# Five double blocks of a top-1 expert layer: first layer with the weights stationary and 256 tokens moving

## The chip, the core and the metric

One core of a Trainium2 chip runs the whole kernel as one launch. The metric is the device time of an execution in microseconds; several executions were timed, and one more was recorded by the hardware profiler.

## The reference

Three stages follow one another: attention with sink and window over 2 x 768 tokens and 8 heads; a mixture of 8 experts in which every token goes through every expert, weighted by a Sinkhorn matrix; and a second mixture in which each token goes to one expert only. The change is in the third stage:

```python
logits = x @ w_gate                      # x: 1536 x 512, 8 experts
expert_idx = np.argmax(logits, axis=1)
...
for e in range(E):
    mask = expert_idx == e
    xe = x[mask]
    h = np.maximum(xe @ w1[e], 0.0)      # first layer, 512 -> 1024
    ye = h @ w2[e]                       # second layer, 1024 -> 512
    out[mask] = gate_w[mask, None] * ye
```

## The kernel before

Every float32 operand of a matmul is kept as two parts, `hi` and `lo` (`lo = x - hi`), and a product is three matmuls into the same PSUM bank (`mm3`, lines 66 to 69): lo x hi, hi x lo, hi x hi. ScalarE (ACT in the rows) writes the hi part, VectorE (DVE) subtracts for the lo part.

**The third stage.** Tokens of one expert are gathered into blocks of 128 rows, numbered `i`. Blocks 0 and 1 belong to the expert with the most tokens. From 2 on blocks come in *turns* of three: 2, 5, 8, 11, 14, 17 stand alone (all but block 2 are *half* blocks of 64 rows, which carry hi and lo side by side in one operand and need two matmuls in place of three), and 3/4, 6/7, 9/10, 12/13, 15/16 are *pairs* (double blocks) with the same expert, so that they share its weights.

For a block the steps are:
- `gather(i)`: an indirect DMA issued on POOL fetches the rows (tile `acc`).
- `xs_trans(i)`: four transposes on TensorE into PSUM (`xst`, in the one buffer `m0`), the hi part by ACT, the lo part by DVE.
- `m2_l1(i, hf)`: half `hf` of the first layer. The token block is the stationary operand, 512 hidden columns of the weights move: 12 matmuls of 512 columns (8 for a half block) into PSUM bank `L0` or `L1`. The result, tokens by hidden, is read out with its ReLU by ACT (hf 0) or DVE (hf 1); for a half block ACT copies one part and DVE adds the other (`both`).
- `h_trans(i)`: eight transposes on TensorE (`h2p`) turn the hidden layer for use as the stationary operand, and ACT and DVE split it again, four parts each a pair.
- `m2_l2(i)`: 24 matmuls of 512 columns (16 for a half block) into `y`; for a half block ACT copies and DVE adds, then ACT scales by the gate, and POOL issues the scatter to the output.

**Weights.** Each expert needs four 1 MB tiles, loaded by SP into four raw buffers. `item_split` splits a tile in two *steps*: each is one ACT copy and one DVE subtraction of 128x1024 (`w_split`). There are 7 slots for split tiles; `spend(n)` issues up to n steps, if the slot is free (`uses`); `ensure` issues what a block needs at once; a finished split issues the load of the tile four places on. A turn uses eight tiles, 16 steps.

The order on every engine is the order in which the code is written (`manual_schedule`), and each engine works its instructions off in that order. The loop of the third stage, lines 1510 to 1525, is the order before:

```python
for i in range(2, NSURE):
    if i + 1 < NSURE:
        drain(m2_l1(i + 1, 0))
    ...
    spend(2 if i % 3 == 0 else 1)
    if i + 1 < NSURE:
        drain(m2_l1(i + 1, 1))
    spend(2)
    if i + 2 < NSURE:
        xs_trans(i + 2)
    spend(1)
    for n, _ in enumerate(m2_l2(i)):
        if n == 4 and i + 1 < NSURE:
            h_trans(i + 1)
```

Of the kernel before, what the change touches and what calls it, by code (L numbers as in the profile page):

```python
# [8 lines left out]
F32 = mybir.dt.float32  # L9
F32R = mybir.dt.float32r  # L10
# [13 lines left out]
def kernel(  # L24
# [62 lines left out]
    x2d = dram.tile([N, DM], F32, name="x2d")  # L87

    accp = ctx.enter_context(tc.tile_pool(name="accp", bufs=1))
    acc = [accp.tile([128, DM], F32, name=f"acc{i}") for i in range(NT)]  # L90
    xp = ctx.enter_context(tc.tile_pool(name="xp", bufs=1))
    hp_a = ctx.enter_context(tc.tile_pool(name="hp_a", bufs=1))
    xh = [xp.tile([128, KD, CH], F32R, name=f"xh{c}") for c in range(NC)]
# [24 lines left out]
    for t in range(NOVER):  # L118
        for j in range(2):
            FIRST[NSURE + 2 * t + j] = NSURE + 2 * t  # L120
            COL[NSURE + 2 * t + j] = 2 * t + j
    HALF = {2 + 3 * u for u in range(1, NONE)}

    def whose(i, rs):
        return [(i, r) for r in rs] if FIRST[i] == i else []
# [606 lines left out]
    def rows(i):  # L732
        return 64 if i in HALF else 128

# [7 lines left out]
    def gather(i):  # L742
# [4 lines left out]
        )  # L747
        xs_t[i] = x

    def xs_trans(i):  # L750
        x = xs_t.pop(i)
        n = rows(i)
        tp = pools["ps"].tile([128, KD, 128], F32, name="xst", tag="m0")[:, :, 0:n]
        for kk in range(KD):
            nc.tensor.transpose(tp[:, kk, :], x[0:n, kk * 128:(kk + 1) * 128], ident[0:n, 0:n])
        if i in HALF:

            st = stile("xsh", i, [128, KD, 128], F32R)
            nc.scalar.activation(st[:, :, 0:n], tp, AF.Copy)
            nc.vector.tensor_tensor(st[:, :, n:128], tp, st[:, :, 0:n].bitcast(F32), op=ALU.subtract)  # L760
            xst[i] = st, None
            return
        th = stile("xsh", i, [128, KD, 128], F32R)
        tl = stile("xsl", i, [128, KD, 128], F32R)
        nc.scalar.activation(th, tp, AF.Copy)
        nc.vector.tensor_tensor(tl, tp, th.bitcast(F32), op=ALU.subtract)
        xst[i] = th, tl

    def mm(out_ap, ah, al, bh, bl, start, stop):
        if al is not None:  # L770
            mm3(out_ap, ah, al, bh, bl, start, stop)
        else:
            nc.tensor.matmul(out_ap, ah, bl, start=start, stop=False)
            nc.tensor.matmul(out_ap, ah, bh, start=False, stop=stop)

    def both(dst, ps):

        nc.scalar.activation(dst, ps[64:128, :], AF.Copy)
        nc.vector.tensor_tensor(dst, ps[0:64, :], dst, op=ALU.add)

    def m2_l1(i, hf):
        if 2 <= i < NSURE:
            ensure(i, hf)
        th, tl = xst[i]
        wh, wl = w_t[pos[i, hf]]
        ps = ps_m.tile([128, HF], F32, name="L", tag=f"L{hf}")
        for kk in range(KD):
            a = None if tl is None else tl[:, kk, :]
            mm(ps, th[:, kk, :], a, wh[:, kk, :], wl[:, kk, :], kk == 0, kk == KD - 1)
            yield  # L790
        used(i, (hf,))
        h = h2[i, hf] = stile(f"h{hf}", i, [128, HF])
        if i in HALF:
            both(h[0:64, :], ps)
        elif hf == 0 or i < 2 or i == NSURE - 1:
            nc.scalar.activation(h, ps, AF.Relu)
        else:
            nc.vector.tensor_scalar(h, ps, 0.0, None, op0=ALU.max)

    def h_trans(i, hfs=(0, 1)):  # L800
        if hfs[0] == 0:
            h2t[i] = []
        for hf in hfs:
            n = rows(i)
            tp = pools["ps"].tile([128, FB, 128], F32, name="h2p", tag=f"y{1 + hf}")[:, :, 0:n]
            h = h2.pop((i, hf))
            for f in range(FB):
                nc.tensor.transpose(tp[:, f, :], h[0:n, f * 128:(f + 1) * 128], ident[0:n, 0:n])
            th = stile(f"hh{hf}", i, [128, FB, 128], F32R)
            if i in HALF:  # L810
                hi = th[:, :, 0:n]
                nc.scalar.activation(hi, tp, AF.Relu)
                nc.vector.scalar_tensor_tensor(
                    th[:, :, n:128], tp, 0.0, hi.bitcast(F32), op0=ALU.max, op1=ALU.subtract
                )
                h2t[i].append((th, None))
                continue
            tl = stile(f"hl{hf}", i, [128, FB, 128], F32R)
            nc.scalar.activation(th, tp, AF.Copy)
            nc.vector.tensor_tensor(tl, tp, th.bitcast(F32), op=ALU.subtract)  # L820
            h2t[i].append((th, tl))

    def m2_l2(i):
        pool, tag = ((ps_m, "y0"), (pools["ps"], "m2"))[i % 2]
        ps = pool.tile([128, DM], F32, name="y", tag=tag)
        for f in range(2 * FB):
            if f % FB == 0 and 2 <= i < NSURE:
                ensure(i, 2 + f // FB)
            th, tl = h2t[i][f // FB]
            wh, wl = w_t[pos[i, 2 + f // FB]]  # L830
            a = None if tl is None else tl[:, f % FB, :]
            mm(ps, th[:, f % FB, :], a, wh[:, f % FB, :], wl[:, f % FB, :], f == 0, f == 2 * FB - 1)
            if f % FB == FB - 1:
                used(i, (2 + f // FB,))
            yield
        y = stile("y", i, [128, DM])[0:rows(i), :]
        if i in HALF:
            both(y, ps)
            ps = y
        nc.scalar.activation(y, ps, AF.Copy, scale=index(g_s, g_d, i))  # L840
        nc.gpsimd.indirect_dma_start(  # L841
            out=out, out_offset=bass.IndirectOffsetOnAxis(ap=index(is_s, is_d, i), axis=0), in_=y, in_offset=None,
            bounds_check=N - 1, oob_is_err=False,
        )
# [4 lines left out]
    def spend(n):  # L849
        while n > 0:  # L850
            if not todo:
                m = head[0]
                if m >= NHEAD or (m >= len(SLOTS) and uses[m - len(SLOTS)] > 0):
                    return
                todo.append(item_split(m))
                head[0] += 1
            try:
                next(todo[0])
                n -= 1
            except StopIteration:  # L860
                todo.pop(0)
# [523 lines left out]
    def tick():  # L1385
        for job in list(jobs):
            job[0] -= 1
            if job[0] <= 0:
                try:
                    w = next(job[1])  # L1390
                    job[0] = 4 if w is None else w
                except StopIteration:
                    jobs.remove(job)

    with tc.manual_schedule():
# [50 lines left out]
        def hand_over():  # L1446
            raw2.extend(p.tile([128, FB, 512], F32, name="raw", tag="raw") for p in (raw_a, raw_b, raw_c, raw_c))
            s0 = (NG - 1) * NC * FB
            hs = [((hp_a if j < 4 else hp_b), j) for j in ((s0 + t) % 6 for t in range(6))]
            free = [(p, f"h{x}{j}") for p, j in hs for x in "hl"]  # L1450
            a = [(accp, f"acc{j}") for j in range(NT)]
            small.update(xs=[a[0], a[1], a[8]], xsh=a[3:5], xsl=a[5:7], R=[a[2], a[7]], y=a[9:11])
            small.update(h0=free[8:12:2], h1=free[9:12:2])
            for j, key in enumerate(("hh0", "hl0", "hh1", "hl1")):
                small[key] = [free[j], free[4 + j]]

        for g in range(NG):
            for c in range(NC):
# [23 lines left out]
        def mix(gen):  # L1482
            for _ in gen:
                tick()
# [5 lines left out]
        for i in range(2):  # L1490
            mix(m2_l1(i, 0))
            for n, _ in enumerate(m2_l1(i, 1)):
                tick()
                if n == 0:
                    h_trans(i, (0,))
            h_trans(i, (1,))
            for n, _ in enumerate(m2_l2(i)):
                tick()
                if n == 5:
                    while i + 1 not in xs_t:  # L1500
                        tick()
                    xs_trans(i + 1)
        mix(m2_l1(2, 0))
        xs_trans(3)
        mix(m2_l1(2, 1))
        while jobs:
            tick()
        h_trans(2)
        spend(4)
        for i in range(2, NSURE):  # L1510
            if i + 1 < NSURE:
                drain(m2_l1(i + 1, 0))
            if i + 3 < NSURE:
                gather(i + 3)
            spend(2 if i % 3 == 0 else 1)
            if i + 1 < NSURE:
                drain(m2_l1(i + 1, 1))
            spend(2)
            if i + 2 < NSURE:
                xs_trans(i + 2)  # L1520
            spend(1)
            for n, _ in enumerate(m2_l2(i)):
                if n == 4 and i + 1 < NSURE:
                    h_trans(i + 1)
            spend(1 if i < NSURE - 2 else 8)
        more = nc.values_load(mo_i[0:1, 0:1], min_val=0, max_val=NOVER)  # L1526

        def over(t):
# [53 lines left out]
```

## Time and profile before

| | us |
|---|---|
| median of 3 timed executions | 1448.63 (1448.29 to 1449.07) |
| the profiled execution, its own time | 1447.51 |
| its span, first to last instruction | 1445.3 |
| TensorE busy in it | 1406.3 |
| VectorE busy | 684.6 |
| ScalarE busy | 454.1 |
| GpSimd (POOL) busy | 130.2 |

The profiled execution's time is its span and 2.2 us around it. Busy times are sums over stages that are very different: attention in the first 200 us, the first expert layer up to about 1210 us, then the routing and the blocks of the second expert layer. PE in the rows is TensorE's matmuls, PEld its weight loads, which lie beside the matmuls. The duration of a matmul in a row reaches to the end of its result and overlaps the next; how often one can follow another is read from the starts.

### The profile page before, as it was taken

How to read it: one execution, taken by the hardware profiler on the slowest of the kernel's cores; microseconds unless marked ns; L12 is line 12 of the kernel's file. 1: busy time of each engine (PE TensorE's matmuls, PEld its weight loads, DVE VectorE, ACT ScalarE, POOL GpSimd, SP SyncE). 2: the span in 40 equal slices, each digit the busy share in tenths (PEclk: the TensorE clock that was granted, in tenths of full speed). 3: DMA queues.
4: the chain of work that ended last, by engine and by line, in shares of the span. 5: the costliest groups of instructions: out<-in, count | busy, mean ns of one | idle time of the engine just before them, and what ended most of it. 6: DMA issues, size and time to landing. Idle time of an engine off the chain costs nothing. (4 is left out here: it accounts for less than half of the span.)

```text
span 1445.3 us, 17989 instructions
## 1 busy us (share of the span) xinstructions
PE 1406.3 (97%) x7101; PEld 1150.3 (80%) x7101; DVE 684.6 (47%) x1369; ACT 454.1 (31%) x895; POOL 130.2 (9%) x172
## 2 busy tenths in 40 slices
PE   7799999999999999999999999999999999899997
PEld 5587887888888888888888888888888877688885
DVE  7777644543333323232433333242323257877884
ACT  5766522021121112020221112020221123477774
POOL 3644400000000000000000000000000000212221
PEclk9999999999999999999999999999999999999999
DMA  6322112010101000010101000010100041797782
GB/s 131 78 59 53 38 59 87 1 59 1 59 0 59 29 29 30 29 59 0 58 0 59 30 30 30 30 58 0 58 1 0 15 161 37 248 319 276 271 291 71
DMA packets 85707, 105.01 MB, mean 73 GB/s; under 512 B 41358, under 2 KB 41358, under 8 KB 85616
## 3 DMA queue, kind: packets, MB, share of 16 engines
q1 hardware_dynamic: 83056, 96.58, 20.2%
q0 software_dynamic: 2560, 7.21, 1.4%
q8 instruction: 58, 0.95, 0.3%
q14 instruction: 33, 0.27, 0.1%
HBM read 100.63 MB, written 7.21 MB: 75 GB/s over the span
## 5 line engine op out<-in xcount | busy, mean ns | idle before, releaser
L210 ACT ACTIVATE hh<-L 128x512 fp32r<-128x512 f32 x192 | 114.7, 597 | 794.9 <-PE L L69 794.8
L211 DVE SCALAR_TENSOR_TENSOR hl<-L,hh 128x512 fp32r<-128x512 f32 x192 | 132.8, 692 | 345.5 <-ACT hh L210 344.8
L235 DVE SCALAR_TENSOR_TENSOR acc<-y,Pm,acc 128x512 f32<-128x512 f32 x168 | 126.1, 751 | 252.3 <-PE y L69 251.9
L67 PE MATMUL y<-whb,hl 128*128 128x512 f32 x416 | 164.8, 396 | 0.0
L67 PE MATMUL y<-wha,hl 128*128 128x512 f32 x412 | 163.2, 396 | 0.0
L69 PE MATMUL y<-whb,hh 128*128 128x512 f32 x416 | 162.2, 390 | 0.0
L68 PE MATMUL y<-wlb,hh 128*128 128x512 f32 x416 | 162.1, 390 | 0.0
L69 PE MATMUL y<-wha,hh 128*128 128x512 f32 x412 | 160.6, 390 | 0.0
L68 PE MATMUL y<-wla,hh 128*128 128x512 f32 x412 | 160.5, 390 | 0.0
L67 PE MATMUL L<-xh,wla 128*128 128x512 f32 x384 | 152.2, 396 | 0.0
L67 PE MATMUL L<-xh,wlb 128*128 128x512 f32 x384 | 150.9, 393 | 0.0
L68 PE MATMUL L<-xl,wha 128*128 128x512 f32 x384 | 149.6, 389 | 0.0
L69 PE MATMUL L<-xh,wha 128*128 128x512 f32 x384 | 149.6, 389 | 0.0
L68 PE MATMUL L<-xl,whb 128*128 128x512 f32 x384 | 149.5, 389 | 0.0
L69 PE MATMUL L<-xh,whb 128*128 128x512 f32 x384 | 149.5, 389 | 0.0
L745 POOL DMA_INDIRECT acc<-x2d,ig_s x2 | 2.1, 1048 | 1044.2 <-DVE tmp_d L458 1019.1
L69 PEld LDWEIGHTS y<-whb,hh 128*128 128x128 f32 x416 | 78.1, 188 | 16.6
L67 PEld LDWEIGHTS y<-whb,hl 128*128 128x128 f32 x416 | 78.1, 188 | 15.7
L67 PEld LDWEIGHTS y<-wha,hl 128*128 128x128 f32 x412 | 77.3, 188 | 16.5 <-issue 0.2
L68 PEld LDWEIGHTS y<-wlb,hh 128*128 128x128 f32 x416 | 78.2, 188 | 15.3
L69 PEld LDWEIGHTS y<-wha,hh 128*128 128x128 f32 x412 | 77.3, 188 | 16.3
L68 PEld LDWEIGHTS y<-wla,hh 128*128 128x128 f32 x412 | 77.4, 188 | 14.8
(346 smaller groups left out, 2297.0 us busy)
## 6 DMA issues: line engine op xcount, KB each, us to landing
raw<-in_moe_w SPq DMA_DIRECT2D x80, 1024.0 KB
raw<-in_v SPq DMA_DIRECT2D x12, 256.0 KB
raw<-vfb SPq DMA_DIRECT2D x12, 256.0 KB
x2d<-acc SPq DMA_DIRECT2D x12, 256.0 KB
raw<-in_k SPq DMA_DIRECT2D x11, 256.0 KB
raw<-in_q SPq DMA_DIRECT2D x11, 256.0 KB
raw<-in_k SPq DMA_DIRECT2D x2, 128.0 KB
raw<-in_q SPq DMA_DIRECT2D x2, 128.0 KB
```

The costliest lines, as they stand in the source:

```text
L67: nc.tensor.matmul(out_ap, al, bh, start=start, stop=False)
L68: nc.tensor.matmul(out_ap, ah, bl, start=False, stop=False)
L69: nc.tensor.matmul(out_ap, ah, bh, start=False, stop=stop)
L210: nc.scalar.activation(hh, ps, AF.Relu)
L211: nc.vector.scalar_tensor_tensor(hl, ps, 0.0, hh.bitcast(F32), op0=ALU.max, op1=ALU.subtract)
L235: nc.vector.scalar_tensor_tensor(a, ps, Pm[:, blk, e:e + 1], a, op0=ALU.mult, op1=ALU.add)
L745: nc.gpsimd.indirect_dma_start(out=x[0:rows(i), :], out_offset=None, in_=src, in_offset=bass.IndirectOffsetOnAxis(ap=index(ig_s, ig_d, i), ...
```

## The change

A pair's first layer is computed with the roles exchanged: 128x128 tiles of the weights are stationary and the 256 tokens of the pair move, so that the result comes out hidden by tokens, as the second layer wants it. A new `pair_l1(i, hf)` does both blocks of a pair at once, in two *units* for each half: 24 matmuls of 256 columns into one bank (`L0`, `L1` in turn), then one ACT ReLU (hi) and one DVE step (lo). The pair has no `h_trans` any more. The hidden tiles of a pair take eight buffers, `xpair` holds the pair's transposed tokens in two tiles of 256 columns (two pairs of `acc` buffers are joined for it). Half blocks and block 2 keep the old form.

The loop is written by *units of work*: the half block's first layer, or the pair's, is issued one place ahead of its second layer; the transposes of the gathered blocks two places ahead; split steps stand behind the pair's units (2 each, 8), in the pair's second layers (3 each, 6), in the half block's second layer (2) and behind its two first-layer halves (1 each, 2).

```diff
+        if i in PAIR or i - 1 in PAIR:
+            js = slice(0, 128) if i in PAIR else slice(128, 256)
+            th, tl = (t[:, :, js] for t in xpair[i if i in PAIR else i - 1])
+            nc.scalar.activation(th, tp, AF.Copy)
+            nc.vector.tensor_tensor(tl, tp, th.bitcast(F32), op=ALU.subtract)
+            return
...
+    def pair_l1(i, hf):
+
+        ensure(i, hf)
+        th, tl = xpair[i]
+        wh, wl = w_t[pos[i, hf]]
+        for u in range(2):
+            ps = ps_m.tile([128, 2, 256], F32, name="L", tag=f"L{u}")
+            for j in range(2):
+                fs = slice((2 * u + j) * 128, (2 * u + j + 1) * 128)
+                for kk in range(KD):
+                    mm3(ps[:, j, :], wh[:, kk, fs], wl[:, kk, fs], th[:, kk, :], tl[:, kk, :], kk == 0, kk == KD - 1)
+            if u == 1:
+                used(i, (hf,))
+                used(i + 1, (hf,))
+            n = 2 * (2 * hf + u)
+            hh, hl = (stile("hp", n + j, [128, 2, 256], F32R) for j in range(2))
+            nc.scalar.activation(hh, ps, AF.Relu)
+            nc.vector.scalar_tensor_tensor(hl, ps, 0.0, hh.bitcast(F32), op0=ALU.max, op1=ALU.subtract)
...
+            yield
...
+        def turn(i):
+
+            xs_trans(i)
+            if i + 3 < NSURE:
+                gather(i + 3)
+
+        gather(5)
         mix(m2_l1(2, 0))
-        xs_trans(3)
+        turn(3)
         mix(m2_l1(2, 1))
         while jobs:
             tick()
+        turn(4)
         h_trans(2)
-        spend(4)
-        for i in range(2, NSURE):
...
+        spend(3)
+        units = [(2,)]
+        for i in sorted(PAIR):
+            units += [(i, i + 1), (i + 2,)]
+        for n, u in enumerate(units):
+            v, w = (units[n + k] if n + k < len(units) else () for k in (1, 2))
+            for hf in range(2):
+                if len(v) == 2:
+                    for _ in pair_l1(v[0], hf):
+                        spend(2)
+                elif v:
+                    drain(m2_l1(v[0], hf))
+                    spend(1)
+                for i in w[hf:hf + 1]:
+                    turn(i)
+            for i in u:
+                for k, _ in enumerate(m2_l2(i)):
+                    if k == 4 and i == u[-1] and len(v) == 1:
+                        h_trans(v[0])
+                    if k in ((1, 3, 6) if len(u) == 2 else (2, 5)):
+                        spend(1)
+            if n == len(units) - 2:
+                spend(8)
```

How this moves instructions, first on TensorE, from the gathered block 9 on. `xst` are the transposes of gathered blocks, `h2p` those of the hidden layer, `L` is the first layer, `y` the second; the number behind a name is that of its buffer's use. Before: xst of block 9, second layer of block 7 with the half block 8's h2p in it, first layer of block 9, xst of block 10, second layer of block 8, in it block 9's h2p (rows that only repeat are left out):

```order
L755 MATMUL xst<-ident,acc_10856 128x128 x4
L67 MATMUL y<-xh_10767,hl_10922 128x512
L68 MATMUL y<-xl_10768,hh_10921 128x512
L69 MATMUL y<-xh_10767,hh_10921 128x512
...
L808 MATMUL h2p<-ident,hh_10959 128x64 x4
L808 MATMUL h2p<-ident,hl_10978 128x64 x4
...
L67 MATMUL L<-wha_10896,acc_10994 128x512
L68 MATMUL L<-wla_10897,acc_10993 128x512
...
L755 MATMUL xst<-ident,acc_10962 128x128 x4
L773 MATMUL y<-xl_10985,hh_11020 128x512
...
L808 MATMUL h2p<-ident,hh_11073 128x128 x4
L808 MATMUL h2p<-ident,hl_11092 128x128 x4
```

Now: the half block 8's xst between the units of the pair 6/7 (256 columns, weights stationary), then, behind the second layer of block 5, the two halves of block 8's first layer, each with one xst of the next pair (block 9, block 10) behind it, and only then block 6's second layer:

```order
L67 MATMUL L<-acc_10624,wla_10596 128x256
L68 MATMUL L<-acc_10625,wha_10595 128x256
L69 MATMUL L<-acc_10624,wha_10595 128x256
L764 MATMUL xst<-ident,acc_10499 128x64 x4
L67 MATMUL L<-acc_10624,wla_10649 128x256
...
L789 MATMUL L<-whb_10885,acc_10850 128x512
L764 MATMUL xst<-ident,acc_10633 128x128 x4
L788 MATMUL L<-wla_10922,acc_10850 128x512
L789 MATMUL L<-wha_10921,acc_10850 128x512
...
L764 MATMUL xst<-ident,acc_10659 128x128 x4
L67 MATMUL y<-xh_10793,hl_10789 128x512
```

What moved: the pair's h2p are gone, and between the two xst, where a whole second layer and a first layer stood, stand eight matmuls (L788 and L789, four times in turn).

Then VectorE at the same place. L177 (now L182) is a split step's subtraction, `x2` two of them; L766 (now L769) is the read of xst. Before, from the half block 8's first-layer sums (L779) to the reads of xst of blocks 9 and 10:

```order
L779 TENSOR_TENSOR hl_10978<-L,hl_10978 64x512
L177 TENSOR_TENSOR xl_10966<-raw,xh_10965 128x1024
L177 TENSOR_TENSOR xl_10985<-raw,xh_10984 128x1024
L766 TENSOR_TENSOR acc_10994<-xst,acc_10993 128x512
L177 TENSOR_TENSOR xl_10985<-raw,xh_10984 128x1024
L813 SCALAR_TENSOR_TENSOR hh_11020<-h2p,hh_11020 128x4x64
L813 SCALAR_TENSOR_TENSOR hh_11028<-h2p,hh_11028 128x4x64
L177 TENSOR_TENSOR xl_11057<-raw,xh_11056 128x1024 x2
L798 TENSOR_SCALAR hl_11092<-L 128x512
L177 TENSOR_TENSOR wlb_11096<-raw,whb_11095 128x1024 x2
L766 TENSOR_TENSOR acc_11107<-xst,acc_11106 128x512
```

Now, from the third unit of pair 6/7 (L813) over block 5's output sum (L794 with `y`) and block 8's first-layer sums (L794 with `L`) to the reads of xst of blocks 9 and 10:

```order
L813 SCALAR_TENSOR_TENSOR hl_10881<-L,hh_10880 128x512
L182 TENSOR_TENSOR wlb_10886<-raw,whb_10885 128x1024 x2
L813 SCALAR_TENSOR_TENSOR acc_10917<-L,acc_10916 128x512
L182 TENSOR_TENSOR wla_10922<-raw,wha_10921 128x1024 x2
L182 TENSOR_TENSOR wla_10936<-raw,wha_10935 128x1024 x2
L794 TENSOR_TENSOR acc_10951<-y,acc_10951 64x512
L794 TENSOR_TENSOR hh_10967<-L,hh_10967 64x512
L182 TENSOR_TENSOR xl_10972<-raw,xh_10971 128x1024
L769 TENSOR_TENSOR acc_10976<-xst,acc_10975 128x4x128
L794 TENSOR_TENSOR hl_10995<-L,hl_10995 64x512
L182 TENSOR_TENSOR xl_10972<-raw,xh_10971 128x1024
L769 TENSOR_TENSOR acc_10976<-xst,acc_10975 128x4x128
```

What moved: six of the split steps stand between the pair's third unit and block 5's output sum, and the two reads of xst have one sum and one split step between them.

## Rows read from the trace of the kernel before

**Rows 1.** The page, part 1: busy us, share of the span, instructions.

```profile
PE 1406.3 (97%) x7101; PEld 1150.3 (80%) x7101; DVE 684.6 (47%) x1369; ACT 454.1 (31%) x895; POOL 130.2 (9%) x172
```

**Rows 2.** Windows, one turn of the second expert layer.

```profile
core 0: us, PE busy (x) PEld busy (x) DVE busy (x) ACT busy (x) POOL busy (x), PEclk, DMA share, GB/s
...
1314.97:1348.24 33.27, 33.27 (x166) 27.20 (x165) 26.22 (x31) 24.44 (x34) 7.37 (x7) 1.00 0.79 288
```

**Rows 3.** Waits in four turns: engine, line, releaser: us in total, times, longest.

```profile
ACT acc L840 <- DVE acc L779: 3.8, 4, 0.9
...
PEld xst L755 <- issue: 1.8, 5, 0.4
```

**Rows 4.** Timeline of PE around block 9's xst: start us, us, engine, line, operation.

```profile
1322.31 0.39 PE L773 MATMUL L<-wlb,acc 128*128 128x512 f32 x1
...
1325.49 0.60 PE L755 MATMUL xst<-ident,acc 128*128 128x128 f32 x4
...
1326.16 0.40 PE L68 MATMUL y<-xl,hh 128*128 128x512 f32 x1
```

**Rows 5.** Timeline of PE, a full block's h2p and what follows.

```profile
1307.19 0.60 PE L808 MATMUL h2p<-ident,hh 128*128 128x128 f32 x4
...
1308.30 0.40 PE L774 MATMUL y<-xh,hh 128*128 128x512 f32 x1
```

**Rows 6.** Timeline of PE in the attention: scores.

```profile
151.01 0.30 PE L68 MATMUL sc<-kl,qh 64*128 64x272 f32 x2
151.14 0.29 PE L69 MATMUL sc<-kh,qh 64*128 64x272 f32 x2
```

**Rows 7.** Timeline of weight loads, four for matmuls of four columns.

```profile
1205.04 0.52 PEld L542 LDWEIGHTS tab<-A,acc 128*128 128x128 f32 x4 [0.57 <-DVE acc L535]
```

**Rows 8.** Timeline of DVE in the second expert layer.

```profile
1267.91 3.49 DVE L177 TENSOR_TENSOR xl<-raw,xh 128x1024 fp32r<-128x1024 f32 x3
...
1319.65 0.42 DVE L760 TENSOR_TENSOR acc<-xst,acc 128x256 fp32r<-128x256 f32 x1
1319.98 1.22 DVE L177 TENSOR_TENSOR wla<-raw,wha 128x1024 fp32r<-128x1024 f32 x1
1321.11 1.28 DVE L820 TENSOR_TENSOR hl<-h2p,hh 128x512 fp32r<-128x512 f32 x2
...
1346.20 1.23 DVE L177 TENSOR_TENSOR wlb<-raw,whb 128x1024 fp32r<-128x1024 f32 x1 [1.74 <-ACT whb L175]
```

**Rows 9.** Timeline of ACT in a turn.

```profile
1315.31 2.00 ACT L175 ACTIVATE wha<-raw 128x1024 fp32r<-128x1024 f32 x2
...
1341.09 1.09 ACT L819 ACTIVATE hh<-h2p 128x512 fp32r<-128x512 f32 x2 [0.96 <-PE h2p L808]
...
1344.49 0.73 ACT L840 ACTIVATE acc<-acc,g_d 64x512 f32<-64x512 f32 x1 [0.94 <-DVE acc L779]
1345.12 1.04 ACT L175 ACTIVATE whb<-raw 128x1024 fp32r<-128x1024 f32 x1
```

**Rows 10.** Timeline of all engines, a half block's first half done.

```profile
1323.67 0.39 PE L773 MATMUL L<-wla,acc 128*128 128x512 f32 x1
...
1323.93 0.60 ACT L778 ACTIVATE hh<-L 64x512 f32<-64x512 f32 x1 [0.19 <-PE L L774]
```

**Rows 11.** Timeline of PE around a half block's xst.

```profile
1314.65 0.39 PE L69 MATMUL L<-wha,acc 128*128 128x512 f32 x1
...
1315.70 0.39 PE L68 MATMUL y<-xl,hh 128*128 128x512 f32 x1
```

**Rows 12.** Timeline of PE, xst of block 2.

```profile
1254.26 0.63 PE L755 MATMUL xst<-ident,acc 128*128 128x128 f32 x4 [2.01 <-DMA acc<-x2d,ig_d]
```

**Rows 13.** Windows with the granted clock, early and ahead of the turns.

```profile
40.00:42.40 2.40, 1.20 (x11) 0.70 (x10) 1.29 (x2) 1.75 (x5) 2.32 (x3) 1.00 0.00 0
42.40:46.00 3.60, 3.60 (x26) 3.27 (x26) 2.18 (x9) 2.82 (x8) 2.86 (x4) 0.53 0.00 0
1240.00:1256.00 16.00, 13.71 (x71) 10.80 (x69) 12.87 (x34) 7.37 (x10) 3.85 (x5) 1.00 1.01 365
```

More of the change, by code (lines that the diff above doesn't have):

```diff
@@ L89 @@
     accp = ctx.enter_context(tc.tile_pool(name="accp", bufs=1))
-    acc = [accp.tile([128, DM], F32, name=f"acc{i}") for i in range(NT)]
+    acc = [None if 3 <= i < 7 else accp.tile([128, DM], F32, name=f"acc{i}") for i in range(NT)]
+    for i in (3, 5):
+        t = accp.tile([128, 2, DM], F32, name=f"acc{i}")
+        acc[i], acc[i + 1] = t[:, 0, :], t[:, 1, :]
     xp = ctx.enter_context(tc.tile_pool(name="xp", bufs=1))
@@ L122 @@
     HALF = {2 + 3 * u for u in range(1, NONE)}
+    PAIR = {3 + 3 * t for t in range(NPAIR)}
     def whose(i, rs):
@@ L748, in gather @@
         xs_t[i] = x
+    xpair = {}
     def xs_trans(i):
@@ L752, in xs_trans @@
         n = rows(i)
+        if i in PAIR:
+            xpair[i] = [stile("xp", j, [128, KD, 256], F32R) for j in range(2)]
         tp = pools["ps"].tile([128, KD, 128], F32, name="xst", tag="m0")[:, :, 0:n]
@@ L779, in both @@
         nc.vector.tensor_tensor(dst, ps[0:64, :], dst, op=ALU.add)
+    def pair_l1(i, hf):
[15 more added lines that the diff above has]
+            nc.vector.scalar_tensor_tensor(hl, ps, 0.0, hh.bitcast(F32), op0=ALU.max, op1=ALU.subtract)
+            for b in range(2):
+                for j in range(2):
+                    h2t.setdefault(i + b, []).append(
+                        (hh[:, j, b * 128:(b + 1) * 128], hl[:, j, b * 128:(b + 1) * 128])
+                    )
+            yield
     def m2_l1(i, hf):
@@ L815, in h_trans @@
                 )
-                h2t[i].append((th, None))
+                h2t[i] += [(th[:, f, :], None) for f in range(FB)]
                 continue
@@ L820, in h_trans @@
             nc.vector.tensor_tensor(tl, tp, th.bitcast(F32), op=ALU.subtract)
-            h2t[i].append((th, tl))
+            h2t[i] += [(th[:, f, :], tl[:, f, :]) for f in range(FB)]
     def m2_l2(i):
@@ L828, in m2_l2 @@
                 ensure(i, 2 + f // FB)
-            th, tl = h2t[i][f // FB]
+            th, tl = h2t[i][f]
             wh, wl = w_t[pos[i, 2 + f // FB]]
-            a = None if tl is None else tl[:, f % FB, :]
-            mm(ps, th[:, f % FB, :], a, wh[:, f % FB, :], wl[:, f % FB, :], f == 0, f == 2 * FB - 1)
+            mm(ps, th, tl, wh[:, f % FB, :], wl[:, f % FB, :], f == 0, f == 2 * FB - 1)
             if f % FB == FB - 1:
@@ L1451, in hand_over @@
             a = [(accp, f"acc{j}") for j in range(NT)]
-            small.update(xs=[a[0], a[1], a[8]], xsh=a[3:5], xsl=a[5:7], R=[a[2], a[7]], y=a[9:11])
-            small.update(h0=free[8:12:2], h1=free[9:12:2])
+            small.update(xs=[a[0], a[1], a[8]], xsh=[a[3], a[3], a[11]], xsl=[a[5], a[5], (pools["s"], "x2h")], R=[a[2], a[7]])
+            small.update(y=a[9:11], h0=free[8:9], h1=free[9:10], xp=[a[3], a[5]])
+            small.update(hp=free[4:8] + free[10:12] + [a[2], a[7]])
             for j, key in enumerate(("hh0", "hl0", "hh1", "hl1")):
-                small[key] = [free[j], free[4 + j]]
+                small[key] = [free[j]]
         for g in range(NG):
@@ L1507 @@
             tick()
+        turn(4)
         h_trans(2)
-        spend(4)
-        for i in range(2, NSURE):
[L1511 to L1525, printed above, removed]
+        spend(3)
[21 more added lines that the diff above has]
+                spend(8)
         more = nc.values_load(mo_i[0:1, 0:1], min_val=0, max_val=NOVER)
```

## Prediction

> **What bounds the kernel now.** I read the page's busy table first: TensorE is busy 1406.3 of 1445.3 us [rows 1], so only what TensorE does, or waits for, can move the end by much. Then the windows, one for each turn of the second expert layer (a half block and the two blocks behind it). A turn takes 33.27 us, TensorE is busy in all of it, VectorE (DVE) in 26.2, ScalarE (ACT) in 24.4, the DMA share is 0.79 [rows 2]. The view of waits over four turns has for TensorE only short "issue" waits of weight loads (1.8 us for xst in four turns); ACT waits 3.8 us in all for DVE, ahead of the scaling of the half blocks' output [rows 3]. So a turn is TensorE's program, with about 7 us of DVE time to spare. The reader is to keep both in mind: a shorter program helps only while DVE and ACT, which work in order, still hand TensorE each buffer in time.
>
> **The change, part by part.**
>
> *Transposes that go.* Ten blocks (3, 4, 6, 7, ... 16) lose the eight h2p transposes. In the timeline the two groups of four begin at 1307.19, and the second matmul behind them at 1308.30; one ordinary matmul (0.23) taken off, the detour cost 1308.30 - 1307.19 - 0.23 = 0.88 us [rows 5]. Ten of them: **-8.8 us**, all of it on TensorE's path.
>
> *The first layer's matmuls.* Ten blocks x 24 matmuls of 512 columns at 0.227 us (14 of them from 1322.31 to 1325.49 [rows 4]) are 54.5 us; they become 480 of 256 columns, each with a 128x128 weight load of its own. No row shows this shape. From below: 0.113, half of the 512. From above: the scores, 272 columns on half the array's rows, come in groups of two matmuls with two loads, 0.13 from one group to the next (151.01 to 151.14 [rows 6]); so 0.130. Between them, the load by itself: four with almost no matmul between take 0.52 us, one alone 0.19, so one comes every 0.11 us [rows 7], less than the matmul beside which it would lie. I take 0.120 (0.13 less 16 of the 272 columns at 0.44 ns, and a little less again, since a group there has two matmuls): 57.6 us, **+3.1 us** (bounds 0 and +7.9).
>
> The load every 0.11 us and the 512-column spacing of 0.227 [rows 4, 7] say that a load lies beside the matmul ahead of it. The Trainium skill (TensorE: Matmul & The Clock Gate, "Part 3: Packing small matmuls") says that a weight load overlaps matmuls in flight only when the row group differs, and these use all rows. By that rule, which speaks against this change, the load would be added; this trace does not agree, since 512 columns would then take over 0.3, against 0.227. What a load that is not hidden would give is the third rival.
>
> *Evictions.* For a pair DVE had 2 evictions of L and 4 of h2p; it has 4 now, ACT likewise. That is 2 x 0.60 us less on DVE a turn (1.28 for two of 0.68 [rows 8]). It is off the path and buys nothing by itself.
>
> *Moved: the gathered blocks' transposes, and the splits.* Before, each xst group has a whole block's second layer or first layer between it and the next. Now the two groups of the next pair stand with only the half block's second eight matmuls, 1.81 us, between them, and both use the one PSUM buffer m0: the second may start only when DVE has read the first. And ahead of them DVE has a new burst: two split steps after each of the pair's four units, two more in the half block's second layer. I walk a middle turn (pair 6/7, half 8, next pair 9/10), with steps start to start: a split 1.13 on DVE (three in 3.49, one 1.23) and 0.95 on ACT (two in 2.00), 512 columns 0.60 and 0.49, a half group 0.33 on DVE (1319.65 to 1319.98) [rows 8, 9]. ACT starts 0.26 us after TensorE's slot ends [rows 10]; DVE starts 1.08 us after ACT starts a split (1345.12 to 1346.20 [rows 8, 9]), so 0.64 after a 512 (0.60 and the same 0.04).
>
> Zero is the end of the pair's second unit; a unit is 24 x 0.120 = 2.88.
> TensorE: half block's xst 0.59 (four small transposes lie between the matmuls at 1314.65 and 1315.70, two of 0.23 taken off [rows 11]), unit 3 ends at 3.47, unit 4 at 6.35, second layer of half block 5 (16 matmuls) at 9.98, first eight of block 8 at 11.79, xst of block 9 (0.44, 1325.49 to 1326.16 less 0.23 [rows 4]) at 12.23, second eight at 14.0. Here xst of block 10 wants to start.
> DVE: unit 1 ended at -2.88, ACT evicted at -2.62, splits on ACT from -2.13, so DVE's two from -1.05 to 1.22. Unit 2's eviction has been ready since 0.9 and runs to 1.82; two splits to 4.09, the half's xst to 4.42, unit 3's eviction (ready 4.37) to 5.03, a split that waits for ACT from 5.30, two to 7.56, unit 4's eviction 8.16, four splits 12.68, half block 5's output sum 13.28. TensorE had finished that output at 9.98: **DVE is late here**, and ACT, in order, stands before the scaling of that output until 13.4. Behind it on ACT: scaling 0.63 (1344.49 to 1345.12 [rows 9]), copy of block 8's first half 14.0 to 14.5, one split to 15.45, copy of block 9's xst. DVE follows: sum 15.2, split 15.6 to 16.7, block 9's xst to 17.3, seen at about 17.5. TensorE waits **3.5 us** at block 10's xst. Behind that wait stand 48 second-layer matmuls (10.9 us) with few splits, in which DVE and ACT catch up, so the wait doesn't grow; it comes back in each turn.
>
> It occurs with pairs 9/10, 12/13, 15/16. Ahead of pair 6/7 the block in the place of half block 5 is block 2, a full one: 8 more matmuls (1.81 us) of cover, so about 1.7 us. After the last pair none follows. Sum of waits 3 x 3.5 + 1.7 = **+12.2 us**. Bounds: below, if DVE never waited for ACT and had nothing left of unit 1, its work from unit 2's eviction to block 9's xst is 9 splits (10.2), six 512 steps (three evictions, two sums, the xst: 3.6) and 0.33, 14.1 us from 0.9, ready at 15.1: 1.1 us a turn, 3.3 in all, none ahead of 6/7. Above, 4 us a turn (a 0.113 matmul brings TensorE to the place 0.3 earlier, and DVE no sooner).
>
> *At no cost:* weight loads, 8 a turn, lie beside the matmuls (share 0.79 of 33.27 is 26 us [rows 2]; a turn stays longer than that); gathers issued earlier on POOL, busy 7.4 us a turn; the first pair's xst of block 4 moved ahead of h2p of block 2. Uncovered, each would be a wait of a microsecond, once.
>
> Sum: -8.8 + 3.1 + 12.2 = **+6.5 us**. The profiled execution took 1447.51 us (span 1445.3 and 2.2 around it), 1.1 less than the median 1448.63; on the median the forecast is **1455.1 us**.
>
> **The rivals.**
>
> *1. DVE is in time (the other side).* If the splits keep up, the change is worth -8.8 + 3.1 = -5.7: 1442.9; with the lower bound of the waits -2.4: 1446.2. It decides at 5.7 us of waits in all, 1.4 at each of four places. For it: DVE has 7 us to spare in a turn, and evictions get fewer. Against: the spare time lies in the 10.9 us behind the wait, and what DVE must do ahead of it is 14.1 us of work. Chance 0.15.
>
> *2. The waits bring the clock down.* At 40 us, after a stretch in which TensorE was busy 1.20 of 2.40 us, the granted clock was 0.53 for 3.6 us (the half level); in 1240 to 1256, with a wait of 2.01 us, it stayed 1.00 [rows 12, 13]. No row has a wait of 3.5 in this stage. At half rate 3.6 us lose 1.7 us, three times 5.1: 1456.8 to 1460.2. Chance 0.22.
>
> *3. The weight load is not hidden at 256 columns.* Each matmul takes 0.11 + 0.11 = 0.22, 480 of them 105.6 us, +51.1 - 8.8 = +42; units then take 5.3 us, DVE is in time and the waits go: about 1491. The 512 rows speak against it. The Trainium skill's rule named above would have it so. Chance 0.03.
>
> **How the numbers follow.** Forecast as worked out, 0.60: with 0.113 and 4-us waits -8.8 + 0 + 13.5 = +4.7 (1453.3), with 0.130 and 12.2 +11.3 (1459.9). The 80% range takes this, most of the clock's case, and the upper part of rival 1: 1448.0 to 1461.0. What this kernel's measurement can tell from no change is about 0.2%, 2.9 us. Faster: two thirds of rival 1, 0.10. Same: the rest of it and a forecast with waits of half the size (+0.4), 0.14. Slower 0.76.
>
> **What would show it.** Right: no h2p rows of the ten blocks; 256-column matmuls 0.12 apart, in units of 2.9 us; TensorE's idle of 3 to 4 us ahead of the second xst group of pairs 9/10, 12/13, 15/16, put down to DVE's read of xst; ACT waiting some 2 us for DVE at the half block's scaling; turns of about 35.4 us instead of 33.27. Wrong: turns near 32.2 with TensorE busy throughout (rival 1), clock below 1.00 behind the waits (2), matmuls 0.19 apart or more (3), or TensorE waiting for a split or a weight load at a unit's start, which I count at nothing.

## The result, and the profile after

The changed kernel took 1457.91 us (median of four executions, 1456.78 to 1459.15); the kernel before, run beside it, 1448.85 (four, 1448.29 to 1449.59). The ratio is 1.0063, with a 95% interval of 1.0051 to 1.0075: slower by 9.1 us, where the forecast was 6.5. The profiled execution after took 1457.53 us with a span of 1455.7, 10.4 more than the span before.

The page of the changed kernel, its span and busy times (before: [rows 1]):

```profile
span 1455.7 us, 18232 instructions
PE 1405.8 (97%) x7261; PEld 1158.5 (80%) x7261; DVE 679.2 (47%) x1359; ACT 449.5 (31%) x885; POOL 128.0 (9%) x172
```

TensorE is as busy as before (1405.8 against 1406.3) while the span is 10.4 us longer, so on balance the time went into TensorE's idle. (Busy time also counts matmuls that a lower clock stretched; as worked out below, that and the shorter program about cancel in it.) The turns, each from the second unit's end of one pair to that of the next, and four stretches inside, as windows of the changed kernel:

```profile
core 0: us, PE busy (x) PEld busy (x) DVE busy (x) ACT busy (x) POOL busy (x), PEclk, DMA share, GB/s
1305.37:1342.23 36.86, 33.68 (x197) 29.23 (x197) 25.29 (x30) 23.52 (x31) 7.34 (x6) 0.95 0.74 261
1342.23:1379.38 37.15, 33.89 (x197) 29.38 (x196) 25.35 (x30) 23.51 (x31) 6.41 (x6) 0.95 0.73 259
1379.38:1416.42 37.04, 33.86 (x198) 29.23 (x197) 25.20 (x30) 23.52 (x31) 4.16 (x4) 0.95 0.69 242
...
1285.60:1296.00 10.40, 9.19 (x43) 7.34 (x43) 7.43 (x8) 6.05 (x8) 2.58 (x2) 1.00 0.96 341
1322.30:1325.70 3.40, 2.98 (x9) 2.57 (x10) 3.03 (x5) 2.52 (x4) 1.74 (x2) 0.50 0.52 166
1359.80:1363.20 3.40, 3.40 (x11) 2.83 (x11) 3.14 (x4) 2.54 (x4) 1.25 (x1) 0.50 0.41 141
1397.40:1400.80 3.40, 3.40 (x9) 2.62 (x9) 3.40 (x4) 2.49 (x3) 0.00 (x0) 0.50 0.31 103
```

A turn of 33.27 us [rows 2] became one of 36.9 to 37.2, and each has two things that it did not have: idle time on TensorE of about 3.2 us, and 3.4 us at the half level of the clock (1.2 of 2.4 GHz). What TensorE waited for, in the view of waits of the changed kernel, from block 2's second layer to the last pair's (us in total, times, longest), and ACT's longest such group in the three turns:

```profile
PE xst L764 <- DVE acc L769: 10.8, 4, 3.3
...
ACT acc L879 <- DVE acc L794: 5.5, 3, 1.8
```

The places are those of the forecast. The timeline of PE around block 10's xst (its start behind eight matmuls of the half block's second half, the wait in brackets):

```profile
1317.08 0.60 PE L764 MATMUL xst<-ident,acc 128*128 128x128 f32 x4
...
1319.14 0.39 PE L789 MATMUL L<-wha,acc 128*128 128x512 f32 x1
1322.71 1.11 PE L764 MATMUL xst<-ident,acc 128*128 128x128 f32 x4 [3.18 <-DVE acc L769]
```

The eighth matmul starts at 1319.14, and 0.23 later block 10's xst could start; it starts at 1322.71, 3.34 us late. Worked out from starts in this way, the waits are 1.37 us ahead of block 7's xst (1285.67 to 1287.27), and 3.34, 3.42 and 3.35 ahead of those of blocks 10, 13 and 16: 11.5 us in all. The brackets say some 0.2 less, since a modelled end of a matmul lies behind its slot.

Why DVE is late is to be read from its own timeline of the changed kernel, from the first pair units on:

```profile
1306.46 0.68 DVE L813 SCALAR_TENSOR_TENSOR hl<-L,hh 128x512 fp32r<-128x512 f32 x1
1307.06 2.36 DVE L182 TENSOR_TENSOR wlb<-raw,whb 128x1024 fp32r<-128x1024 f32 x2
...
1313.39 4.63 DVE L182 TENSOR_TENSOR wla<-raw,wha 128x1024 fp32r<-128x1024 f32 x4
1317.94 0.68 DVE L794 TENSOR_TENSOR acc<-y,acc 64x512 f32<-64x512 f32 x1
1319.89 0.68 DVE L794 TENSOR_TENSOR hh<-L,hh 64x512 f32<-64x512 f32 x1 [1.27 <-ACT hh L793]
1320.83 1.23 DVE L182 TENSOR_TENSOR xl<-raw,xh 128x1024 fp32r<-128x1024 f32 x1 [0.26 <-ACT xh L180]
1321.98 0.68 DVE L769 TENSOR_TENSOR acc<-xst,acc 128x512 fp32r<-128x512 f32 x1
```

Four splits in a row hold the output sum (L794 with `y`) until 1317.94. ACT, which works in order, waits for that sum, then scales, copies, and splits; DVE in turn waits 1.27 and 0.26 us for ACT; and block 9's xst, finished about 1317.7 (1317.08 and its 0.60), is read at 1321.98. ACT at the same place:

```profile
1318.65 0.72 ACT L879 ACTIVATE acc<-acc,g_d 64x512 f32<-64x512 f32 x1 [1.83 <-DVE acc L794]
1319.28 0.58 ACT L793 ACTIVATE hh<-L 64x512 f32<-64x512 f32 x1
1319.76 1.04 ACT L180 ACTIVATE xh<-raw 128x1024 fp32r<-128x1024 f32 x1
```

Last, the price of the 256-column matmuls, from the timeline of PE in a unit of the changed kernel:

```profile
1306.45 0.28 PE L69 MATMUL L<-acc,wha 128*128 128x256 f32 x1
1306.57 0.28 PE L67 MATMUL L<-acc,wla 128*128 128x256 f32 x1
1306.69 0.28 PE L68 MATMUL L<-acc,wha 128*128 128x256 f32 x1
```

They follow each other every 0.12 us, each with a weight load of its own.

### The profile page after: what moved, and what is told of

The parts are those of the page before. It is cut to its first block, busy times and chain, and to the rows that moved or that the text cites. A ratio compares the mean times of both kernels' runs of the same rounds, so it can differ in the third digit from the quotient of the medians.

```text
span 1455.7 us, 18232 instructions
## 1 busy us (share of the span) xinstructions
PE 1405.8 (97%) x7261; PEld 1158.5 (80%) x7261; DVE 679.2 (47%) x1359; ACT 449.5 (31%) x885; POOL 128.0 (9%) x172
## 5 line engine op out<-in xcount | busy, mean ns | idle before, releaser
L67 PE MATMUL y<-wha,hl 128*128 128x512 f32 x404 | 159.7, 395 | 0.0
L69 PE MATMUL y<-wha,hh 128*128 128x512 f32 x404 | 157.4, 389 | 0.0
L68 PE MATMUL y<-wla,hh 128*128 128x512 f32 x404 | 157.3, 389 | 0.0
```

What stands on the lines that cost most here:

```text
L67: nc.tensor.matmul(out_ap, al, bh, start=start, stop=False)
L68: nc.tensor.matmul(out_ap, ah, bl, start=False, stop=False)
```

## Experiments

The theory: the shorter program is worth -5.7 us (-8.8 + 3.1); the waits at the second xst cost 11.5; and behind each long wait of this profile the clock falls, which costs some 1.6 more each. A rival leaves the clock out and lays the rest on slower matmuls or late weights; another holds that the wait, if removed, comes back elsewhere. Durations are medians, with the kernel before run beside them on the same chip.

**The second xst in another bank.** `m1` is a PSUM buffer that no step of the turns uses (the routing ahead of them does); the second xst of a pair (not the first pair's) goes there, so that it need not wait for the read of the first. Order and work stay the same.

```diff
-        tp = pools["ps"].tile([128, KD, 128], F32, name="xst", tag="m0")[:, :, 0:n]
+        tp = pools["ps"].tile([128, KD, 128], F32, name="xst", tag="m1" if i - 1 in PAIR and i > 4 else "m0")[:, :, 0:n]
```

> The changed kernel, with one edit: the second xst group of a pair (blocks 7, 10, 13, 16) goes to another PSUM buffer (m1), so that it need not wait until DVE has read the first. Theory A (DVE is late, the one buffer turns that into TensorE's wait, and the wait brings the clock down): no wait of TensorE over 0.3 us at any of the four places, no fall of the clock in the turns, turns near 32 us, the whole 5 to 6 us below the kernel before (-8.8 + 3.1), ratio 0.996. Theory B (DVE and ACT have no time to spare in a turn of this length, so a wait taken away comes back at the next buffer): turns stay at 35 us or more, the wait stands at L, y or a split, ratio above 1.002.

Measured: 1442.26 us (1441.84 to 1443.28) against 1448.55, ratio 0.9952 (0.9939 to 0.9966). Windows of the three turns, and the timeline of PE at block 10's xst, of this kernel:

```profile
1306.05:1338.09 32.04, 32.04 (x197) 28.16 (x196) 25.17 (x30) 23.53 (x31) 6.85 (x6) 1.00 0.88 301
1338.09:1370.14 32.05, 32.05 (x198) 28.16 (x197) 25.16 (x30) 23.53 (x31) 6.83 (x6) 1.00 0.87 298
1370.14:1402.18 32.04, 32.04 (x197) 28.16 (x196) 25.09 (x30) 23.53 (x31) 4.80 (x4) 1.00 0.83 281
```

```profile
1319.82 0.39 PE L789 MATMUL L<-wha,acc 128*128 128x512 f32 x1
1320.05 0.60 PE L764 MATMUL xst<-ident,acc 128*128 128x128 f32 x4
```

The xst follows in 0.23 us; TensorE waits for nothing in the turns, and the clock stays at 1.00 there. The wait does not come back elsewhere. A turn without waits is 32.04 us, 1.23 less than before, which answers to the forecast's -8.8 + 3.1 for the whole (-5.7; measured -6.3). It also gives the price of the clock in the changed kernel: its three turns are 4.82, 5.11 and 5.00 us above 32.04, and 3.34, 3.42 and 3.35 of that are waits; 1.5, 1.7 and 1.65 are left, where 3.4 us at half rate lose 1.7, if TensorE has work all the while.

**The second xst at another place.** The other way to remove the wait: block 10's xst (and its like) moves from behind the half block's second half into the pair's second layer, four steps in.

```diff
                 for i in w[hf:hf + 1]:
-                    turn(i)
+                    if hf == 0:
+                        turn(i)
             for i in u:
                 for k, _ in enumerate(m2_l2(i)):
+                    if k == 4 and i == u[0] and len(w) == 2:
+                        turn(w[1])
```

> The changed kernel with the second xst group of each next pair moved: no longer behind the half block's first layer, but behind the fifth step of the second layer of the pair's first block, 15 matmuls (3.4 us) later; the one PSUM buffer stays. Theory A (TensorE waits only because the place comes 3.4 us before DVE has read the first group): the waits at xst of blocks 7, 10, 13, 16 fall to 0.2 us or less, the clock stays up in the turns, turns of 32.0 to 32.2 us, 5 to 6 us below the kernel before, as with two buffers. If DVE's lateness is only put off, the wait comes back there or at the pair's first unit, which needs this group's tokens, and the time stays above the kernel before.

Measured: 1443.34 us (1442.29 to 1444.42) against 1448.48, ratio 0.9961 (0.9947 to 0.9975). The first turn's window and all of TensorE's waits from 1270 us on, of this kernel:

```profile
1303.00:1335.00 32.00, 32.00 (x197) 27.95 (x197) 25.18 (x28) 23.54 (x31) 9.04 (x6) 1.00 0.87 300
```

```profile
PE xst L764 <- DVE acc L769: 0.4, 1, 0.4
```

With one buffer, but a longer stretch between its two uses, the wait is gone as well, but for 0.4 us once, and the turn is the same 32.0. So it is the nearness of the two uses of `m0`, not the amount of DVE's work, that cost the time.

**The wait filled with other matmuls.** Fourteen matmuls of 512 columns, whose result nobody reads, go where TensorE would wait; they take the wait's time and keep TensorE busy.

```diff
+        def fill(i, k):
+            ps = pools["ps"].tile([128, 512], F32, name="fil", tag="m1")
+            th = xst[i][0]
+            wh = w_t[pos[i, 1]][0]
+            for j in range(k):
+                nc.tensor.matmul(ps, th[:, j % KD, :], wh[:, j % KD, :], start=j == 0, stop=j == k - 1)
...
                     drain(m2_l1(v[0], hf))
+                    if hf == 1 and n >= 3 and w:
+                        fill(v[0], 14)
```

> The changed kernel with 14 more matmuls of 512 columns (3.2 us, result unused) ahead of the second xst of pairs 9/10, 12/13, 15/16, where TensorE waits 3.4 us. They do no useful work and fill the wait only. Theory A (the wait lowers the clock, and this costs 1.7 us each time): the clock stays at its upper level in the turns, the xst begins where it did, and the whole is about 5 us faster than the changed kernel, near 1453. Theory C (the fall of the clock costs nothing, since DVE sets the pace of the turn anyhow, or it is not the wait that brings it): no faster than the changed kernel, 1457 to 1459.

Measured: 1453.9 us (1453.56 to 1455.57) against 1448.55, ratio 1.0037 (1.0023 to 1.005). Windows of two turns, and the timeline of PE, of this kernel:

```profile
1306.02:1341.48 35.46, 35.46 (x211) 30.72 (x211) 25.19 (x30) 23.51 (x31) 7.80 (x6) 1.00 0.79 271
1341.48:1377.01 35.53, 35.45 (x211) 30.72 (x210) 25.27 (x30) 23.51 (x31) 6.75 (x6) 1.00 0.80 271
```

```profile
1320.02 3.35 PE L1554 MATMUL fil<-wha,acc 128*128 128x512 f32 x14
1323.37 0.66 PE L764 MATMUL xst<-ident,acc 128*128 128x128 f32 x4
```

The xst comes as late as in the changed kernel (3.35 us), the work of the turn is the same, and yet each of the three turns is 1.4 to 1.6 us shorter, with the clock at 1.00 in all of them. This separates wait and clock: over its own kernel before, the filled kernel is 5.35 us slower, the changed one 9.06 (and 9.82 in the repeat below), so the clock's share is 3.7 to 4.5 us. The share is a rough one, since the clock also falls elsewhere: the filled kernel's profile has 6.8 us at half level in the routing, at 1230.7, where the changed kernel's profiles have none. The timed executions point the same way by their mean granted clock: 0.988 to 0.993 in the nine of the changed kernel, 0.993 to 0.996 in the five of the filled one, 0.992 to 0.996 in 24 of the kernel before.

**The half block's splits moved.** The two split steps in the half block's second layer go to the pair's second layers, where DVE has time.

```diff
-                    if k in ((1, 3, 6) if len(u) == 2 else (2, 5)):
+                    if k in ((1, 2, 3, 6) if len(u) == 2 else ()):
```

> The changed kernel, with the two split steps in the half block's second layer moved into the pair's second layers (four a block there in place of three). Theory A (it is the burst of splits on DVE ahead of the half block's output sum that makes DVE late): two steps of 1.13 us and the hold of ACT go from ahead of the wait, which falls from 3.4 to about 1.7 us in the three later turns; ACT no longer waits 2 us at the scaling. With waits so short the clock should stay up, and the whole comes to within 2 us of the kernel before. If the place of the splits is of no account, the waits stay at 3.4 us and the time at 9 us above the kernel before. A new wait may come in the first turn, for weights of block 5.

Measured: 1449.22 us (11 executions, 1447.94 to 1450.41) against 1448.55, ratio 1.0002 (0.9993 to 1.0011). TensorE's waits in this kernel, block 2's second layer to the end of the turns:

```profile
PE xst L764 <- DVE acc L769: 4.3, 3, 1.5
PE L L788 <- DVE wlb L182: 1.6, 1, 1.6
```

From starts the xst waits are 1.56, 1.64 and 1.56 us, 1.8 less than in the changed kernel; no fall of the clock follows them (turns of 33.68 and 33.74 at 1.00). A new one of 1.75 stands ahead of the second half of block 5, whose weights are now split later. -5.7 + 4.8 + 1.75 = +0.8 us; measured +0.7. Two splits fewer in the burst are worth half of the wait and the whole of the clock's fall.

**The splits spread evenly.** One step behind each of the pair's units in place of two, five in each second layer of the pair.

```diff
                     for _ in pair_l1(v[0], hf):
-                        spend(2)
+                        spend(1)
...
-                    if k in ((1, 3, 6) if len(u) == 2 else (2, 5)):
+                    if k in ((0, 2, 3, 5, 7) if len(u) == 2 else (2, 5)):
```

> The changed kernel with the 16 split steps of a turn spread evenly: one behind each of the pair's four units in place of two, five in each of the pair's second layers in place of three, the half block's as they are. DVE is then in time at the half block's output sum, and the wait at the second xst should go. But the half block's first-layer weights are split later: two or four steps behind their place, waits of 0.7 and about 3 us at the half block's first layer. So Theory A expects no gain: the wait only moves from xst to L, turns of 35.5 us, 4 to 12 us above the kernel before. If splits are ready early enough in any order, the waits go and the time falls below the kernel before by 5 us.

Measured: 1459.56 us (four executions, 1459.35 to 1461.17) against 1448.55, ratio 1.0075 (1.006 to 1.0091). TensorE's waits in the three turns of this kernel, and its timeline at one of them:

```profile
PE L L788 <- DVE wla L182: 4.7, 2, 2.4
```

```profile
1322.29 0.40 PE L789 MATMUL L<-wha,acc 128*128 128x512 f32 x1
1325.05 0.50 PE L788 MATMUL L<-wla,acc 128*128 128x512 f32 x1 [2.36 <-DVE wla L182]
```

The waits at xst are gone, but the half block's second half now waits for its split weights: from starts 2.20 and 1.76 us at the first half block, then 2.53, 2.54, 2.53 and, at the last, 2.95 (expected were 0.7 and about 3 at each half block; from the second half block on there is one wait at each). The clock fell behind one of them (turn 36.28, against 34.68 for the two others). -5.7 + 14.5 + 1.6 = +10.4, where the medians differ by 11.0. The burst of eight steps that makes the read of xst late is thus what keeps the weights in time; thinning it moves the stall, and doesn't remove it.

**The changed kernel again.** Without an edit, five executions more.

> The changed kernel once more, unedited, on the same chip as the run with the moved xst. Theory A expects the three waits of 3.3 to 3.5 us at the second xst, a fall of the clock behind each, and 9 us above the kernel before, ratio 1.006.

Measured: 1458.3 us (1457.3 to 1459.85) against 1448.48, ratio 1.0069 (1.0055 to 1.0083). The waits are the same from starts, 1.37 and three of 3.34. Windows behind them, in this profile:

```profile
1286.00:1297.00 11.00, 9.79 (x45) 7.83 (x45) 7.65 (x8) 6.46 (x10) 2.85 (x3) 1.00 0.92 309
1322.80:1329.60 6.80, 6.04 (x17) 4.90 (x18) 5.48 (x7) 3.52 (x5) 2.09 (x2) 0.50 0.74 254
1357.00:1366.00 9.00, 5.82 (x28) 4.56 (x27) 7.46 (x10) 6.78 (x9) 4.54 (x3) 1.00 0.88 272
1397.90:1401.30 3.40, 3.40 (x10) 2.66 (x10) 3.40 (x4) 2.49 (x3) 0.00 (x0) 0.50 0.23 45
```

The same wait was followed by 6.8 us at half level, by none, and by 3.4: the fall is likely behind such a wait, not certain. Over both profiles it came behind five of six.

## Why the prediction was right, and where it was off

**Transposes that go, and the first layer's matmuls:** right. The 0.120 us taken between 0.113 and 0.130 is what the rows show, and the two kernels without waits are worth -6.3 and -5.1 us, around the forecast's -5.7. With this spacing the third rival falls: a load that was not hidden would have made it 0.22. The Trainium skill (TensorE: Matmul & The Clock Gate, "Part 3: Packing small matmuls") says in its list of what overlaps that a weight load overlaps matmuls in flight only where the row group differs; this trace does not agree with that line, since all of these use all rows and follow each other every 0.12 us, where a load added to each would have made 0.22.

**The walk along DVE and ACT:** right to 0.1 us at every step set beside it. Counted from the second unit's end (1305.28: its last matmul starts at 1305.16, and 0.12 follow), the changed kernel has the second eviction at 1.18 (forecast 1.22), the output sum at 12.66 (12.68), the scaling at 13.37 (13.4), the read of block 9's xst at 16.70 (16.7), and block 10's xst at 17.43 (17.5), with TensorE ready at 14.09 (14.0).

**The waits, 12.2 us:** 11.5. Three came out at 3.3 to 3.4 in place of 3.5, the first at 1.37 in place of 1.7. The first rival (DVE in time) fell with that. The turn of 35.4 us that was named as a sign is 35.6 by the forecast's own terms (33.27 - 1.76 + 0.62 + 3.5); the measured 36.9 to 37.2 have the clock's 1.5 to 1.7 in them.

**The clock** is where the forecast was off. The sum left it out, and the second rival had it at 0.22; it came behind all three long waits of the profiled execution, and the sizes given for it there (1.7 each, 1456.8 to 1460.2) hold the result. The step that failed is the weight, not the working: one wait of 2.01 us without a fall [rows 12, 13] was read as speaking against it, although nothing there was as long as 3.5 us. Even that wait is a weak witness: at the same place, block 2's xst, the eight profiles wait 1.99 to 2.46 us from starts, and behind one of these waits (2.42, in the kernel with the moved xst) the clock did fall, for 3.4 us from 1255.2.

The account of the profiled execution is -8.8 + 3.1 + 11.5 + 4.8 = +10.6 us, against 10.4 between the spans. The medians differ by 9.1: the profiled execution before was 1.3 us under the median of the runs beside the changed one, the profiled one after 0.4 under its own, and the time around the span was 2.2 us before and 1.8 after.

**At no cost:** right in the changed kernel (no unit waits for a weight or a gather); the two kernels with splits moved show how near that was.

What stays open: what decides whether the clock falls behind a wait of 3.3 us, since it once did not.

## What to carry to other kernels

A free engine's share of busy time says little about a wait: walk the in-order queues of the engines that hand over a buffer, operation by operation from the traced start-to-start times, from the last point at which all are free; here that found the three long waits to 0.2 us, and the short first one to 0.3, before anything ran. When a change brings two uses of one PSUM buffer nearer together, give the second its own buffer, or place it where the reader has caught up: a one-line edit turned this change from 9 us slower into 6.3 us faster. Price a long wait in a dense stage of TensorE with a fall of the clock behind it: here, behind waits of 3.3 to 3.4 us, about half as much again, while waits up to 1.8 us in the turns cost nothing more.

## What the runs showed of the hardware that was not expected

Behind waits of 3.3 to 3.4 us in an otherwise full stage TensorE's granted clock fell to its half level in five of six cases, for 3.4 us (once 6.8), and cost 1.5 to 1.7 us a time in the profiled execution; behind waits of 2.2 to 2.95 us in the turns it fell in one of five, and behind those up to 1.8 us there never. Falls also came and went in code that no edit touched: the profile of the kernel with two banks has one in the routing that the profile before and the two of the changed kernel do not have there (those of the filled kernel and of the moved half-block splits have it too):

```profile
1232.00:1238.80 6.80, 6.59 (x18) 5.36 (x19) 5.50 (x30) 0.00 (x0) 0.96 (x1) 0.50 0.16 41
```

It is 6.8 us at half level. Up to block 2's xst the seven profiles with the change run the same code, and that xst starts between 1254.07 and 1256.17 us: single executions are 2 us apart before the turns begin, whether by the clock alone is not shown, and so medians are compared above.
